# Group normalisation on one core: the next tile's mean ahead of this tile's variance, and the last two stores cut into pieces by rows

## The chip, the core and the metric

The kernel runs on one core of one Trainium2 chip. The metric is the device time of one execution in microseconds (us). Before the change the median of two runs is 732.78 us (732.75 and 732.81). The profile is that of one execution: it lasted 732.78 us, of which the span from the first to the last instruction is 731.1 us.

The engines that matter are TensorE (PE), VectorE (DVE), ScalarE (ACT), and SyncE (SP), which only issues transfers here. Sixteen DMA engines move the data. Each engine works through its own list of instructions in order; semaphores make one engine wait for another.

## What is computed

```python
def reference(x, g, b):
    G = 32
    B, C, H, W = x.shape          # 128, 1024, 32, 16, bfloat16
    xr = x.reshape(B, G, C // G, H, W)
    mu = xr.mean(axis=(2, 3, 4), keepdims=True)
    var = ((xr - mu) ** 2).mean(axis=(2, 3, 4), keepdims=True)
    xn = (xr - mu) / jnp.sqrt(var + 1e-5)
    xn = xn.reshape(B, C, H, W)
    return xn * g[None, :, None, None] + b[None, :, None, None]
```

Each of the 128 samples has 32 groups of 32 channels with 512 pixels each, so one group is 16,384 numbers. Mean and variance are taken over a group; scale and shift go by channel.

## The kernel before

A tile is four samples: 4 x 32 groups make 128 rows (partitions), and a row is one whole group of 16,384 bfloat16 numbers, 32 KB. A tile is thus 4 MB, and there are `NT` = 32 of them. Everything a row needs is in that row. Rows of a tile stand behind one another in memory, in the input as in the output.

The work on tile i is cut into steps, each a small function:

- `L(i)` (line 81) loads the tile into a buffer `xt`, one DMA of 128 rows, issued by SP. There are six such buffers (`XBUFS`), and the first six loads are issued at the start.
- `M(i)` (line 121) is 32 matmuls on PE against the unit matrix `eye`, each on 512 columns of the tile, all added up in one PSUM buffer `ps` of 128 x 512 numbers: the row sum is folded 32 to 1. There are three such buffers.
- `R(i)` (line 137) is one DVE instruction that sums `ps` along the row and gives the negative mean `negmean`. It appears with a second short instruction that reads the accumulator.
- `Q(i)` (line 156) is four ACT instructions on 4,096 columns each. They square x - mean and sum, into the four columns of `sq`.
- `V(i)` turns `sq` into scale and shift: DVE sums the four columns (`jv`, line 173), ACT takes the root (`rstd`, line 186), DVE takes the reciprocal (line 190) and forms `scl` (line 195) and `bia` (line 201), 32 channels each.
- `A(i)` (line 218) is 32 DVE instructions, one for each channel: x times scale plus shift, in place in `xt`.
- `S(i)` (line 229) stores the tile, one DMA of 128 rows, issued by SP.

The order on each engine is written out by hand: `chain` ties each instruction to the one before it on its engine. The main loop goes over the tiles and writes, for tile i: `Q(i)`, `V(i)`, `M(i+1)`, then the first 12 instructions of `A(i)` (`A_HEAD`), then `R(i+1)`, then the other 20 of `A(i)`, then `S(i)`, and then the load `L(i+5)` from i = 1 on. So on DVE the mean of the next tile stands inside the normalisation of this one, behind its first 12 instructions. On ACT `Q(i+1)` stands behind the root of `V(i)`; it reads `negmean` of tile i+1. On SP a store and a load alternate; `S(i)` waits for the last instruction of `A(i)`, and `L(i+5)` goes into the buffer that `S(i-1)` empties, so it waits for that store to land.

Of the kernel before, what the change touches and what calls it, by code (L numbers as in the profile page):

```python
# [18 lines left out]
AHEAD = 5  # L19
MM_FREE = 512  # L20
SQ_FREE = 4096
A_HEAD = 12


@with_exitstack
def kernel(
# [8 lines left out]
    nc = tc.nc  # L35
    P = nc.NUM_PARTITIONS
# [6 lines left out]
    NT = B0 // NS  # L43
    KC = C // G
# [8 lines left out]
    o_v = out.rearrange("(t n) (g k) h w -> t (n g) (k h w)", n=NS, g=G)  # L53
# [16 lines left out]
    def chain(key, inst):  # L70
        prev = last.get(key)
        if prev is not None:
            tc.add_manual_dep(inst.ins, prev.ins.name, nosync, reason="pipeline order")
        last[key] = inst
        return inst

    state = {}

    def L(i):
        xt = xpool.tile([P, F], BF16, name="xt")  # L80
        chain("sp", nc.sync.dma_start(out=xt[:], in_=x_v[i]))
        state[i] = {"xt": xt}
# [11 lines left out]
    for n in range(NS):  # L94
# [7 lines left out]
        out=eye[:],  # L102
        in_=ones_b[:],
# [11 lines left out]
    def M(i):  # L115
        st = state[i]
        ps = pspool.tile([P, MMN], F32, name="ps")
        for k in range(NMM):
            chain(
                "pe",  # L120
                nc.tensor.matmul(  # L121
                    out=ps[:],
                    lhsT=eye[:],
                    rhs=st["xt"][:, k * MMN : (k + 1) * MMN],
                    start=(k == 0),
                    stop=(k == NMM - 1),
                ),
            )
        st["ps"] = ps

    def R(i):
        st = state[i]
        negmean = spool.tile([P, 1], F32, name="negmean")
        jd = jpool.tile([P, MMN], BF16, name="jd")
        chain(
            "dve",
            nc.vector.tensor_scalar(  # L137
                out=jd[:],
                in0=st["ps"][:],
                scalar1=-inv_n,  # L140
                scalar2=None,
                op0=ALU.mult,
                op1=ALU.add,
                accum_out=negmean[:],
            ),
        )
        st["negmean"] = negmean

    def Q(i):
        st = state[i]  # L150
        sq = spool.tile([P, NSQ], F32, name="sq")
        for k in range(NSQ):
            ja = jpool.tile([P, SQ_FREE], BF16, name="ja")
            chain(
                "act",
                nc.scalar.activation(  # L156
                    out=ja[:],
                    in_=st["xt"][:, k * SQ_FREE : (k + 1) * SQ_FREE],
                    func=ACT.Square,
                    bias=st["negmean"][:],  # L160
                    scale=1.0,
                    accum_out=sq[:, k : k + 1],
                ),
            )
        st["sq"] = sq

    def V(i):
        st = state[i]
        var = spool.tile([P, 1], F32, name="var")
        jv = spool.tile([P, NSQ], F32, name="jv")  # L170
        chain(
            "dve",
            nc.vector.tensor_scalar(  # L173
                out=jv[:],
                in0=st["sq"][:],
                scalar1=inv_n,
                scalar2=None,
                op0=ALU.mult,
                op1=ALU.add,
                accum_out=var[:],  # L180
            ),
        )
        rstd = spool.tile([P, 1], F32, name="rstd")
        chain(
            "act",
            nc.scalar.activation(  # L186
                out=rstd[:], in_=var[:], func=ACT.Sqrt, bias=eps_t[:], scale=1.0
            ),
        )
        chain("dve", nc.vector.reciprocal(out=rstd[:], in_=rstd[:]))  # L190
        scl = spool.tile([P, KC], F32, name="scl")
        bia = spool.tile([P, KC], F32, name="bia")
        chain(
            "dve",
            nc.vector.tensor_scalar(  # L195
                out=scl[:], in0=gam[:], scalar1=rstd[:], scalar2=None, op0=ALU.mult
            ),
        )
        chain(
            "dve",  # L200
            nc.vector.scalar_tensor_tensor(  # L201
                out=bia[:],
                in0=scl[:],
                scalar=st["negmean"][:],
                in1=bet[:],
                op0=ALU.mult,
                op1=ALU.add,
            ),
        )
        st["scl"], st["bia"] = scl, bia  # L210

    def A(i, lo, hi):
        st = state[i]
        xt = st["xt"]
        for k in range(lo, hi):
            chain(
                "dve",
                nc.vector.tensor_scalar(  # L218
                    out=xt[:, k * HW : (k + 1) * HW],
                    in0=xt[:, k * HW : (k + 1) * HW],  # L220
                    scalar1=st["scl"][:, k : k + 1],
                    scalar2=st["bia"][:, k : k + 1],
                    op0=ALU.mult,
                    op1=ALU.add,
                ),
            )

    def S(i):
        chain("sp", nc.sync.dma_start(out=o_v[i], in_=state[i]["xt"][:]))
        state.pop(i)  # L230

    M(0)
    R(0)
    for i in range(NT):
        Q(i)
        V(i)
        if i + 1 < NT:
            M(i + 1)
        A(i, 0, A_HEAD)
        if i + 1 < NT:  # L240
            R(i + 1)
        A(i, A_HEAD, KC)
        S(i)
        j = i + AHEAD
        if UPFRONT <= j < NT:
            L(j)
# [30 lines left out]
```

## Time and profile before

| | |
|---|---|
| median of two runs | 732.78 us |
| the profiled execution | 732.78 us |
| its span, first to last instruction | 731.1 us |
| ACT busy | 497.5 us, 68% |
| DVE busy | 379.8 us, 52% |
| PE busy | 288.9 us, 40% |
| read from HBM, written to HBM | 134.23 MB, 134.22 MB |
| the transfers' share of 16 DMA engines | 88.7% |

The page names for each group of instructions the line, the engine, the operation, what it writes and reads, how often it ran, its busy time, the mean duration of one in ns, and behind the second bar how long the engine had been idle before it and what ended that. Idle time counts only where the engine in question is the one that others wait for. The small instructions of the variance, which the prediction does not show again, look like this in the costliest groups of the page:

```profile
L173 DVE TENSOR_SCALAR_CACHE_REDUCE jv<-sq 128x4 f32<-128x4 f32 x32 | 5.0, 157 | 293.1 <-ACT ja L156 293.1
L137 DVE TENSOR_SCALAR_CACHE_REDUCE jd<-ps 128x512 bf16<-128x512 f32 x32 | 21.8, 680 | 0.0
L186 ACT ACTIVATE rstd<-var,eps_t 128x1 f32<-128x1 f32 x32 | 9.4, 294 | 7.4 <-DVE jv L173 7.4
```

The last part of the page tells of the DMAs, with the median time from the issue on the queue to the landing of the last byte:

```profile
xt<-in_x_dram SPq DMA_DIRECT2D x32, 4096.0 KB, 21.9
out_dram<-xt SPq DMA_DIRECT2D x32, 4096.0 KB, 12.1
```

### The profile page before, as it was taken

To read this page: it belongs to the slowest core of one execution; us is meant where nothing else is said; L and a number is where in the kernel's file an instruction comes from. 1 tells how busy PE (TensorE), PEld (TensorE's weight loads), DVE (VectorE), ACT (ScalarE), POOL (GpSimd) and SP (SyncE) were. 2 spreads that over 40 slices of the span, in tenths; PEclk is the share of its full clock that TensorE was granted. 3 is DMA by queue.
4 is the path that set the end of the run, shared out by engine and by line. 5 is a ranking of instruction groups with operands and counts; after the bars stand their busy time and mean duration, and the time that the engine had idled before them with its cause. 6 is when DMAs were issued, how large, how long until landed. Compare 5 with 4: busy or idle time off the path is not lost.

```text
span 731.1 us, 3814 instructions
## 1 busy us (share of the span) xinstructions
PE 288.9 (40%) x1024; PEld 113.1 (15%) x1024; DVE 379.8 (52%) x1252; ACT 497.5 (68%) x290; POOL 0.5 (0%) x5
## 2 busy tenths in 40 slices
PE   2874532455543334445323455433344443330000
PEld 0331110122111111112111122111111111110000
DVE  0034466654446665444566544456654445665443
ACT  0267876666787666678766667876666787666670
POOL 0000000000000000000000000000000000000000
PEclk9997656666667667776667766677767776675555
DMA  9998599999999999999999999999999999934555
GB/s 377 431 437 364 229 385 390 403 402 377 397 404 402 373 402 401 402 375 402 402 374 402 402 402 372 403 402 402 373 420 385 378 400 398 401 145 202 229 229 229
DMA packets 9622, 268.70 MB, mean 368 GB/s; under 512 B 1408, under 2 KB 1408, under 8 KB 1408
## 3 DMA queue, kind: packets, MB, share of 16 engines
q1 hardware_dynamic: 9216, 268.44, 88.7%
q8 instruction: 8, 0.13, 0.1%
q14 instruction: 14, 0.11, 0.0%
q10 hardware_dynamic: 384, 0.02, 0.0%
HBM read 134.23 MB, written 134.22 MB: 367 GB/s over the span
## 4 chain that ended last, share of the span: by engine, by line
ACT 68%; DVE 25%; DMA 4%; issue 1%; ACTq 0%; DVEq 0%
ACT ja L156 67%; DVE xt L218 18%; DVE jd L137 3%; DMA bet_b<-in_b_dram 3%; DMA xt<-in_x_dram 2%; ACT rstd L186 1%; DVE bia L201 1%; DVE scl L195 1%; DVE jv L173 1%; DVE rstd L190 1%; ACTq L156 0%; DVEq L272 0%; DVE bet L113 0%
## 5 line engine op out<-in xcount | busy, mean ns | idle before, releaser
L156 ACT ACTIVATE ja<-xt,negmean 128x4096 bf16<-128x4096 bf16 x128 | 474.7, 3708 | 202.2 <-DVE jd L137 199.1
L121 PE MATMUL ps<-xt,eye 128*128 128x512 bf16 x1024 | 288.9, 453 | 356.7 <-DMA xt<-in_x_dram 343.9
L218 DVE TENSOR_SCALAR xt<-xt,scl,bia 128x512 bf16<-128x512 bf16 x1024 | 335.9, 403 | 1.2
L121 PEld LDWEIGHTS <-eye 128*128 128x128 bf16 x1024 | 113.1, 113 | 532.0 <-DMA xt<-in_x_dram 343.4
L173 DVE TENSOR_SCALAR_CACHE_REDUCE jv<-sq 128x4 f32<-128x4 f32 x32 | 5.0, 157 | 293.1 <-ACT ja L156 293.1
L156 ACT ACTIVATION_READ_ACCUMULATOR ja<-xt,negmean 128x1 f32 x128 | 23.9, 187 | 0.0
L137 DVE TENSOR_SCALAR_CACHE_REDUCE jd<-ps 128x512 bf16<-128x512 f32 x32 | 21.8, 680 | 0.0
L186 ACT ACTIVATE rstd<-var,eps_t 128x1 f32<-128x1 f32 x32 | 9.4, 294 | 7.4 <-DVE jv L173 7.4
L112 DVE CAST gam<-gam_b 128x32 f32<-128x32 bf16 x1 | 0.2, 181 | 26.9 <-DMA gam_b<-in_g_dram 26.9
L190 DVE RECIPROCAL rstd<-rstd 128x1 f32<-128x1 f32 x32 | 5.3, 164 | 11.6 <-ACT rstd L186 11.6
L201 DVE SCALAR_TENSOR_TENSOR bia<-scl,negmean,bet 128x32 f32<-128x32 f32 x32 | 8.0, 251 | 1.1
L195 DVE TENSOR_SCALAR scl<-gam,rstd 128x32 f32<-128x32 f32 x32 | 7.7, 242 | 1.1
L173 DVE DVE_READ_ACCUMULATOR jv<-sq 128x1 f32 x32 | 2.6, 83 | 0.0
L137 DVE DVE_READ_ACCUMULATOR jd<-ps 128x1 f32 x32 | 2.5, 79 | 0.0
L113 DVE CAST bet<-bet_b 128x32 f32<-128x32 bf16 x1 | 0.2, 181 | 3.4 <-DMA bet_b<-in_b_dram 3.4
L90 ACT ACT_TABLE_LOAD x1 | 1.3, 1283 | 0.8 <-PEq L261 0.8
L88 DVE MEMSET eps_t<- 128x1 f32 x1 | 0.1, 59 | 0.9 <-PEq L261 0.9
L101 POOL TENSOR_SCALAR_AFFINE_SELECT eye<-ones_b 128x128 bf16<-128x128 bf16 x1 | 0.3, 293 | 0.7 <-DVE ones_b L99 0.7
L90 ACT ACTIVATE warm<-eps_t 128x1 f32<-128x1 f32 x1 | 0.2, 202 | 0.0
L99 DVE MEMSET ones_b<- 128x128 bf16 x1 | 0.2, 165 | 0.0
L261 POOL MEMSET const-bfloat16-1.0<- 128x1 bf16 x1 | 0.1, 101 | 0.0
L261 POOL MEMSET const-uint8-127<- 128x1 uint8 x1 | 0.1, 101 | 0.0
(2 smaller groups left out, 0.2 us busy)
## 6 DMA issues: line engine op xcount, KB each, us to landing
xt<-in_x_dram SPq DMA_DIRECT2D x32, 4096.0 KB, 21.9
out_dram<-xt SPq DMA_DIRECT2D x32, 4096.0 KB, 12.1
gam_b<-in_g_dram ACTq DMA_DIRECT2D x4, 2.0 KB, 15.7
bet_b<-in_b_dram ACTq DMA_DIRECT2D x4, 2.0 KB, 17.1
```

The lines of the kernel that those rows point to most:

```text
L90: chain("act", nc.scalar.activation(out=warm[:], in_=eps_t[:], func=ACT.Sqrt))
L99: nc.vector.memset(ones_b[:], 1.0)
L101: nc.gpsimd.affine_select(out=eye[:], in_=ones_b[:], pattern=[[-1, P]], compare_op=ALU.is_equal, fill=0.0, base=0, channel_multiplier=1,)
L121: nc.tensor.matmul(out=ps[:], lhsT=eye[:], rhs=st["xt"][:, k * MMN : (k + 1) * MMN], start=(k == 0), stop=(k == NMM - 1),),
L137: nc.vector.tensor_scalar(out=jd[:], in0=st["ps"][:], scalar1=-inv_n, scalar2=None, op0=ALU.mult, op1=ALU.add, accum_out=negmean[:],),
L156: nc.scalar.activation(out=ja[:], in_=st["xt"][:, k * SQ_FREE : (k + 1) * SQ_FREE], func=ACT.Square, bias=st["negmean"][:], scale=1.0, acc ...
L173: nc.vector.tensor_scalar(out=jv[:], in0=st["sq"][:], scalar1=inv_n, scalar2=None, op0=ALU.mult, op1=ALU.add, accum_out=var[:],),
L186: nc.scalar.activation(out=rstd[:], in_=var[:], func=ACT.Sqrt, bias=eps_t[:], scale=1.0),
L190: chain("dve", nc.vector.reciprocal(out=rstd[:], in_=rstd[:]))
L195: nc.vector.tensor_scalar(out=scl[:], in0=gam[:], scalar1=rstd[:], scalar2=None, op0=ALU.mult),
L201: nc.vector.scalar_tensor_tensor(out=bia[:], in0=scl[:], scalar=st["negmean"][:], in1=bet[:], op0=ALU.mult, op1=ALU.add,),
L218: nc.vector.tensor_scalar(out=xt[:, k * HW : (k + 1) * HW], in0=xt[:, k * HW : (k + 1) * HW], scalar1=st["scl"][:, k : k + 1], scalar2=st[ ...
```

## The change

Two things are changed. In the main loop, `M(i+1)` and `R(i+1)` now stand ahead of `V(i)`, and `A(i)` is one piece again. In `S`, the stores of the last two tiles are cut into pieces by rows: 112, 7, 5 and 4 rows for tile 30, and 112, 6, 3, 2 and 5 rows for tile 31. What is computed is the same, and so is the number of instructions on PE, DVE and ACT.

```diff
-A_HEAD = 12
...
-    def A(i, lo, hi):
+    def A(i):
         st = state[i]
         xt = st["xt"]
-        for k in range(lo, hi):
+        for k in range(KC):
...
     def S(i):
-        chain("sp", nc.sync.dma_start(out=o_v[i], in_=state[i]["xt"][:]))
+        cuts = {NT - 2: (112, 119, 124, P), NT - 1: (112, 118, 121, 123, P)}.get(i, (P,))
+        lo = 0
+        for hi in cuts:
+            chain(
+                "sp",
+                nc.sync.dma_start(
+                    out=o_v[i][lo:hi, :], in_=state[i]["xt"][lo:hi, :]
+                ),
+            )
+            lo = hi
         state.pop(i)
...
     for i in range(NT):
         Q(i)
-        V(i)
         if i + 1 < NT:
             M(i + 1)
-        A(i, 0, A_HEAD)
-        if i + 1 < NT:
             R(i + 1)
-        A(i, A_HEAD, KC)
+        V(i)
+        A(i)
         S(i)
```

On DVE, from the mean of tile 0 to the variance of tile 1, the order before is this (line 137 is the mean, 173 the first step of the variance, 218 the normalisation; "x12" stands for twelve in a row):

```order
L137 TENSOR_SCALAR jd,negmean<-ps 128x512
L173 TENSOR_SCALAR jv,var<-sq 128x4
L190 RECIPROCAL rstd<-rstd 128x1
L195 TENSOR_SCALAR scl<-gam,rstd 128x32
L201 SCALAR_TENSOR_TENSOR bia<-scl,negmean,bet 128x32
L218 TENSOR_SCALAR xt<-xt,scl,bia 128x512 x12
L137 TENSOR_SCALAR jd,negmean<-ps 128x512
L218 TENSOR_SCALAR xt<-xt,scl,bia 128x512 x20
L173 TENSOR_SCALAR jv,var<-sq 128x4
```

The same stretch of DVE now, where all lines of the kernel are one lower:

```order
L136 TENSOR_SCALAR jd,negmean<-ps 128x512 x2
L172 TENSOR_SCALAR jv,var<-sq 128x4
L189 RECIPROCAL rstd<-rstd 128x1
L194 TENSOR_SCALAR scl<-gam,rstd 128x32
L200 SCALAR_TENSOR_TENSOR bia<-scl,negmean,bet 128x32
L217 TENSOR_SCALAR xt<-xt,scl,bia 128x512 x32
L136 TENSOR_SCALAR jd,negmean<-ps 128x512
L172 TENSOR_SCALAR jv,var<-sq 128x4
```

The mean of tile 1 has moved ahead of the variance of tile 0 (the "x2"), and the mean of tile 2 stands between the normalisation of tile 0 and the variance of tile 1.

On SP, the end of the program now, from the store of tile 26 on, reads as follows; before, the last row of it was five stores of 128 rows:

```order
L233 DMA out_dram<-xt 128x16384
L80 DMA xt<-in_x_dram 128x16384
L233 DMA out_dram<-xt 128x16384 x3
L233 DMA out_dram<-xt 112x16384
L233 DMA out_dram<-xt 7x16384
L233 DMA out_dram<-xt 5x16384
L233 DMA out_dram<-xt 4x16384
L233 DMA out_dram<-xt 112x16384
L233 DMA out_dram<-xt 6x16384
L233 DMA out_dram<-xt 3x16384
L233 DMA out_dram<-xt 2x16384
L233 DMA out_dram<-xt 5x16384
```

Two DMAs have become nine; the stores and loads ahead of them stand as they did.

## The prediction

> **What bounds the kernel now.** I read the chain of work that ended last first, then the costliest groups, then one tile on DVE and ACT in the timeline, and only then the DMA engines. The line of the chain by engine, and three groups:
>
> ```profile
> ACT 68%; DVE 25%; DMA 4%; issue 1%; ACTq 0%; DVEq 0%
> ...
> L156 ACT ACTIVATE ja<-xt,negmean 128x4096 bf16<-128x4096 bf16 x128 | 474.7, 3708 | 202.2 <-DVE jd L137 199.1
> L121 PE MATMUL ps<-xt,eye 128*128 128x512 bf16 x1024 | 288.9, 453 | 356.7 <-DMA xt<-in_x_dram 343.9
> L218 DVE TENSOR_SCALAR xt<-xt,scl,bia 128x512 bf16<-128x512 bf16 x1024 | 335.9, 403 | 1.2
> ```
>
> ACT is 68% of the chain, and the squares (line 156) sat idle for 199.1 us because the mean (line 137, DVE) came late. The DVE share of the chain, 25%, is what stands ahead of that mean. One tile in the timeline, DVE first, then ACT (start, duration, instruction; idle time before it and its releaser in brackets):
>
> ```profile
> 47.76 0.16 DVE L173 TENSOR_SCALAR_CACHE_REDUCE jv<-sq 128x4 f32<-128x4 f32 x1 [15.37 <-ACT ja L156]
> ...
> 49.05 3.97 DVE L218 TENSOR_SCALAR xt<-xt,scl,bia 128x512 bf16<-128x512 bf16 x12
> 52.93 0.68 DVE L137 TENSOR_SCALAR_CACHE_REDUCE jd<-ps 128x512 bf16<-128x512 f32 x1
> ...
> 53.54 6.54 DVE L218 TENSOR_SCALAR xt<-xt,scl,bia 128x512 bf16<-128x512 bf16 x20
> 69.04 0.16 DVE L173 TENSOR_SCALAR_CACHE_REDUCE jv<-sq 128x4 f32<-128x4 f32 x1 [8.96 <-ACT ja L156]
> ```
> ```profile
> 32.42 3.71 ACT L156 ACTIVATE ja<-xt,negmean 128x4096 bf16<-128x4096 bf16 x1 [30.12 <-DVE jd L137]
> ...
> 36.26 3.71 ACT L156 ACTIVATE ja<-xt,negmean 128x4096 bf16<-128x4096 bf16 x1
> ...
> 47.95 0.29 ACT L186 ACTIVATE rstd<-var,eps_t 128x1 f32<-128x1 f32 x1 [0.23 <-DVE jv L173]
> 53.71 3.71 ACT L156 ACTIVATE ja<-xt,negmean 128x4096 bf16<-128x4096 bf16 x1 [5.46 <-DVE jd L137]
> ```
>
> A tile takes 69.04 - 47.76 = 21.28 us, and it is one serial loop: squares 15.33 us on ACT (32.42 to 47.76), variance 1.29 us (47.76 to 49.05), twelve normalisations 3.97, the mean 0.68, and the squares of the next tile. ACT stands idle 5.46 us before them. The DMA engines are nearly full beside that loop. Three windows of the trace (columns: the engines' busy us, PE clock, the mean busy share of 16 DMA engines, GB/s): loads alone, the steady middle, one store alone:
>
> ```profile
> 14.00:38.00 24.00, 21.28 (x80) 8.65 (x79) 0.97 (x4) 5.55 (x3) 0.00 (x0) 0.93 1.01 433
> ...
> 170.00:584.00 414.00, 179.14 (x634) 69.91 (x632) 228.97 (x756) 300.16 (x176) 0.00 (x0) 0.71 0.96 394
> 719.00:731.00 12.00, 0.00 (x0) 0.00 (x0) 0.12 (x1) 0.00 (x0) 0.00 (x0) 0.50 0.82 350
> ```
>
> The middle has a share of 0.96 already. So I expect a gain in the middle of the few per cent that the DMA engines have left, and the larger part at the ends, where they have room.
>
> **Mean ahead of variance.** No instruction is added or taken away on PE, DVE or ACT. `R(i+1)`, 0.68 us, runs while ACT is still squaring tile i, when DVE is idle (8.96 us in the row above). Behind the squares there remain the first step of the variance and the root, then the next squares: a tile would cost ACT 15.33 + (48.26 - 47.76) = 15.8 us. DVE needs 0.7 + 1.3 + 3.97 + 6.54 = 12.5 us, so it is not the bound; that no longer 12 but all 32 normalisations lie beside the squares costs nothing, since 20 of them did before at 6.54 / 20 = 0.327 us each against 3.97 / 12 = 0.331 alone. A compute loop of 15.8 us is faster than the DMA engines, so the next wait is for loads: the step is set by one store and one load, 8.39 MB.
>
> The change adds a wait too. `R(i+1)` needs `M(i+1)` and so load i+1; behind it on DVE stand `V(i)` and `A(i)`, and behind these `S(i)` and `L(i+5)` on SP. A normalisation in one piece and the matmuls behind the last load:
>
> ```profile
> 708.70 10.42 DVE L218 TENSOR_SCALAR xt<-xt,scl,bia 128x512 bf16<-128x512 bf16 x32
> ```
> ```profile
> 636.87 8.73 PE L121 MATMUL ps<-xt,eye 128*128 128x512 bf16 x32 [12.64 <-DMA xt<-in_x_dram]
> ```
>
> From the landing of load i+1 to the issue of load i+5 that is about 8.7 (matmuls) + 0.7 + 1.3 + 10.4, or 21 us; with the 21.8 us of the next store and load (below) 43 us for four tiles, against four steps of over 80. It doesn't bind.
>
> **How long is the step of a full queue?** Before shows no queue that holds stores and loads throughout; I bound it. One pair in the middle (12.1 is its store, 21.4 its load), the issues of the first store and of the last, and how long the last took:
>
> ```profile
> L229 SPq DMA_DIRECT2D out_dram<-xt x1: 332/332/332, 145.2 to 145.2; - x1
> L81 SPq DMA_DIRECT2D xt<-in_x_dram x1: 383/383/383, 145.6 to 145.6; - x1
> ...
> DMA to landing us min/median/max: 12.1/16.7/21.4
> ```
> ```profile
> 60.11 0.34 SPq L229 DMA_DIRECT2D out_dram<-xt  x1
> ```
> ```profile
> 719.15 0.33 SPq L229 DMA_DIRECT2D out_dram<-xt  x1
> ```
> ```profile
> DMA to landing us min/median/max: 11.1/11.1/11.1
> ```
>
> From the store's issue to the load's landing 145.6 + 21.4 - 145.2 = 21.8 us pass. A store alone takes 11.1, while 4.19 MB at the 433 GB/s of loads alone take 9.7, so 1.4 us are latency that a queue hides: the pair moves in 20.4 us. The share gives the same: 0.96 x 21.28 = 20.4. Lower bound: 2 x 9.7 = 19.4, with no loss where a store gives way to a load. Upper bound: 21.8, nothing hidden. I take 20.5, nearest to the two readings, with 0.1 for the turn from load to store.
>
> To that comes one late DMA engine. Matmuls of tiles 2, 3 and 4 start as their loads land, and instruction fetches are in the DMA table:
>
> ```profile
> 32.84 8.65 PE L121 MATMUL ps<-xt,eye 128*128 128x512 bf16 x32 [2.72 <-DMA xt<-in_x_dram]
> 43.98 7.08 PE L121 MATMUL ps<-xt,eye 128*128 128x512 bf16 x32 [2.50 <-DMA xt<-in_x_dram]
> 53.71 8.47 PE L121 MATMUL ps<-xt,eye 128*128 128x512 bf16 x32 [2.64 <-DMA xt<-in_x_dram]
> ```
> ```profile
> q8 instruction: 8, 0.13, 0.1%
> ```
> ```profile
> q8 instruction: 1, 0.02, 4.0%
> ```
>
> The second of these rows is from a window of 39.0 to 40.7 us, the first from the whole page. 9.73 us is the step of 53.71; that of 43.98 is 11.14, and the packet of queue 8 fell into it. So a fetch makes one DMA engine some 1.4 us late, and it stays late while the queue is full. Eight fetches in 32 tiles are one in four: 0.35 us a tile if they always meet the same engine, 0 if they spread. Before, the pause between pairs took that up. I take the full 0.35, since a load has landed only with its last engine: a step of 20.85 us.
>
> **The two stores in pieces.** 128 rows on 16 engines are 8 rows each, 9.7 / 8 = 1.2 us a row. The 112 rows are 7 each. If the 16 other rows meet idle engines, the fullest still has 8: cost 0. If the four small pieces of the last store all begin on the same engine, it has 11: +3.7. If the engine that is late has 7 rows twice, it saves up to 2 x 1.2 = 2.4. So from -2.4 to +3.7; I take +2.0, nearer to the upper end, since small pieces that start alike pile up and lateness is caught up partly while nothing is loaded. Nine issues for two, 0.33 us of SP each, lie beside the transfers. [...]
>
> **The sum**, on the profiled execution. ACT is free of tile 0 at 48.26; squares of tile 1 to 63.6, variance to 64.9, normalisation (10.42) to 75.3.
>
> - Store of tile 1 issued at 75.4. From there 26 pairs (tiles 1 to 26 with loads 6 to 31) of 20.85 = 542.1, and 1.4 of latency: load 31 lands at 618.9 (before 636.9, when the last matmuls start).
> - Tile 31: matmuls 8.7, mean 0.7, squares 15.4, variance 1.3, normalisation 10.4 = 36.5: its store is issued at 655.4. Stores 27 to 30 (4 x 9.7) are through on the late engine at about 658, on the others well before.
> - That store 11.1, pieces 2.0: 668.5. Before, 719.15 + 11.1 = 730.2 stands against a span of 731.1: 0.9 more. The execution's 732.78 is 1.7 over its span, and equals the median of the runs. Together 671.1, so **671 us**.
>
> Where the 62 us come from: store 1 goes out 6 us earlier (before, 60.1 + 21.28 = 81.4), 26 steps give 26 x 0.43 = 11, and after the last load 36.5 us replace the 719.15 - 636.87 = 82.3 in which before still worked off its backlog; the pieces take 2 back.
>
> **Rivals.** (1) A full queue loses nothing and the fetches spread: a step of 19.4 gives 671 - 26 x 1.45 = 633. The 433 GB/s of loads alone speak for it; the pair's 21.8 us against it. (2) Queues that are never empty cost more: fetches of the other engines also hit, or engines drift apart. A step of 21.3 to 22.5 gives 683 to 714. The late load above speaks for it; against it that before keeps 21.28 with a pause in every step. (3) Not faster: with stores and loads always both in flight, the mixed rate falls. Faster ends at 718 us, so at a step of 22.7, or 370 GB/s; slower by 2%, 747 us, begins at 23.8, or 353 GB/s. The place would be the middle, the price 26 times the excess. The windows, with 394 GB/s at 96%, speak against it. [...] (4) The new wait of `V(i)` for load i+1 binds: the loop above would have to be twice as long; the step would stay near 21.3 or more, and the time 683 or over. That the edit does nothing is excluded by the order of DVE's instructions, which has changed.
>
> **How the numbers follow.** Forecast 0.72 (650 to 685 us), rival 1 0.12 (625 to 650), rival 2 with 4 0.11 (685 to 718), rival 3 0.05. The range takes the forecast and the near parts of both neighbours, 645 to 688. Two per cent is about what a measurement of this kernel can tell from no change: faster 0.95, same 0.03 and slower 0.02, these two from rival 3.
>
> **What would show it.** Right: idle time before the squares released by the mean's late matmuls, hence by loads; in the middle a DMA share at or above 1.0, near 405 GB/s, and the landing times of stores and loads grown by the queue; the chain no longer alternating ACT and DVE but with DMA as its largest part; load 31 near 619 and store 31 issued 36 us after it. Wrong: a step of 21 us or more with the share below 0.97 (the compute loop still bound), or the last store's pieces landing over 15 us after its first issue.

## The result, and the profile after

| | before | changed |
|---|---|---|
| median | 732.78 us (2 runs) | 657.25 us (657.0 and 657.5) |
| ratio, with 95% interval | 1 | 0.8969 [0.8948, 0.8991] |
| span of the profiled execution | 731.1 us | 655.3 us (execution 657.0) |
| DMA share of the 16 engines, 170 to 584 us | 0.96 | 1.00 |

The change makes the kernel 10.3% faster. The forecast was 671, the range 645 to 688. The time lies inside it, but two terms of the sum were off, in opposite directions: by -26 and by +12 us. Most of what follows is about these two.

The chain of the changed kernel by engine, and the groups that answer to those shown of before:

```profile
DMA 61%; ACT 21%; PE 8%; DVE 4%; issue 1%; DVEq 0%; SPq 0%
...
L155 ACT ACTIVATE ja<-xt,negmean 128x4096 bf16<-128x4096 bf16 x128 | 474.2, 3704 | 33.0 <-DVE jd L136 29.9
...
L136 DVE TENSOR_SCALAR_CACHE_REDUCE jd<-ps 128x512 bf16<-128x512 f32 x32 | 22.0, 688 | 157.2 <-PE ps L120 149.5
L185 ACT ACTIVATE rstd<-var,eps_t 128x1 f32<-128x1 f32 x32 | 9.4, 294 | 90.6 <-DVE jv L172 90.6
```

ACT's idle time before the squares has shrunk from 202.2 to 33.0 us, and 29.9 of these are one wait at the start of the program. The mean itself now waits, 149.5 us for matmuls, which wait for loads. Since the variance stands behind that mean on DVE, ACT's remaining wait has moved to the root: 90.6 us, for 7.4 before. The chain no longer changes between ACT and DVE; 61% of it is DMA. SP's own waits say what the DMAs wait for (who waited for whom, us in total, times, longest):

```profile
SPq L80 <- DMA out_dram<-xt: 407.0, 24, 19.8
```

A load has to wait until the store before last has emptied its buffer. Before, that store had landed by then, and SP's wait was for the normalisation (670.8 us for the 32 stores; 168.8 now). In the middle the queue is never empty. The windows of the end and of the middle (the last two columns are the DMA share and GB/s):

```profile
598.00:654.00 56.00, 3.60 (x17) 1.45 (x15) 23.10 (x76) 15.69 (x10) 0.00 (x0) 0.58 0.69 262
170.00:584.00 414.00, 195.32 (x659) 76.00 (x672) 250.79 (x827) 328.42 (x193) 0.00 (x0) 0.70 1.00 431
```

431 GB/s with stores and loads mixed is the rate of loads alone (433). The end is poor: 0.69 and 262 GB/s from 598 us on. Behind the last load, the chain in order of time, and the issue of the last store's five pieces on SP:

```profile
592.62 3.17 PE ps L120 x7
...
619.26 6.87 DVE xt L217 x21
```
```profile
L233 SPq DMA_DIRECT2D out_dram<-xt x5: 261/1187/1905, 629.7 to 638.7; - x5
```

Load 31 lands at 592.6, 26 us earlier than forecast. The first piece of the last store goes out at 629.7, 37.1 us later (forecast: 36.5). The last piece lands at 655.3 - 0.9 = 654.4, so the last store took 24.7 us; 13.1 were forecast, and a whole store on idle engines takes 11.1. SP needed 0.26 to 1.9 us for each of the five issues, where the prediction had 0.33; they went out over 9 us.

### The profile page after: what moved, and what is told of

Read it like the earlier page. It is cut to its first block, busy times and chain, and to the rows that moved or that the text cites. A ratio compares the mean times of both kernels' runs of the same rounds, so it can differ in the third digit from the quotient of the medians.

```text
span 655.3 us, 3802 instructions
## 1 busy us (share of the span) xinstructions
PE 288.2 (44%) x1004; PEld 113.7 (17%) x1024; DVE 380.2 (58%) x1252; ACT 494.1 (75%) x290; POOL 0.5 (0%) x5
## 4 chain that ended last, share of the span: by engine, by line
DMA 61%; ACT 21%; PE 8%; DVE 4%; issue 1%; DVEq 0%; SPq 0%
DMA out_dram<-xt 30%; DMA xt<-in_x_dram 29%; ACT ja L155 21%; PE ps L120 8%; DVE xt L217 3%; DMA bet_b<-in_b_dram 3%; DVE jd L136 1%; DVE jv L172 0%; ACT rstd L185 0%; DVE bia L200 0%; DVE scl L194 0%; DVE rstd L189 0%; DVEq L278 0%; DVE bet L112 0%; SPq L80 0%
## 5 line engine op out<-in xcount | busy, mean ns | idle before, releaser
L155 ACT ACTIVATE ja<-xt,negmean 128x4096 bf16<-128x4096 bf16 x128 | 474.2, 3704 | 33.0 <-DVE jd L136 29.9
L136 DVE TENSOR_SCALAR_CACHE_REDUCE jd<-ps 128x512 bf16<-128x512 f32 x32 | 22.0, 688 | 157.2 <-PE ps L120 149.5
L185 ACT ACTIVATE rstd<-var,eps_t 128x1 f32<-128x1 f32 x32 | 9.4, 294 | 90.6 <-DVE jv L172 90.6
## 6 DMA issues: line engine op xcount, KB each, us to landing
xt<-in_x_dram SPq DMA_DIRECT2D x32, 4096.0 KB, 29.9
```

The lines of the kernel that those rows point to most:

```text
L136: nc.vector.tensor_scalar(out=jd[:], in0=st["ps"][:], scalar1=-inv_n, scalar2=None, op0=ALU.mult, op1=ALU.add, accum_out=negmean[:],),
L155: nc.scalar.activation(out=ja[:], in_=st["xt"][:, k * SQ_FREE : (k + 1) * SQ_FREE], func=ACT.Square, bias=st["negmean"][:], scale=1.0, acc ...
L185: nc.scalar.activation(out=rstd[:], in_=var[:], func=ACT.Sqrt, bias=eps_t[:], scale=1.0),
```

## The experiments

**The two parts apart.** The new order with whole stores:

```diff
-        cuts = {NT - 2: (112, 119, 124, P), NT - 1: (112, 118, 121, 123, P)}.get(i, (P,))
...
+        chain("sp", nc.sync.dma_start(out=o_v[i], in_=state[i]["xt"][:]))
```

> The changed order with whole stores, no cuts. In the changed kernel's trace load 31 lands at 592.6 us and the last store is issued at 629.7 but lands at 654.4, with many packets of 2.4 us, twice the usual 1.21, from the moment the first piece of 112 rows moves. Theory A (the cuts slow the transfers beside them): whole stores go at 9.7 us each, so the late DMA engine is through five of them at 592.6 + 5 x 9.7 = 641.1 and the time is 641.1 + 0.4 + 0.9 + 1.7 = 644 us. Theory B (only rows count: the late engine, which had 19 rows of the last two tiles where 16 are its share, saves three rows): 657.2 - 3 x 1.21 = 653.6 us. Theory C (the cuts help): over 657 us. As predicted (the pieces cost 2.0): 655 us.

Measured: 643.99 us (642.96 to 644.84), ratio 0.8787 [0.8774, 0.8800]. Theory A. The last load lands about where it did in the changed kernel, the last store is issued 1.5 us later, and it takes 11.1 us again (the chain, then the store on SP with its time to landing):

```profile
593.42 9.69 PE ps L120 x32
```
```profile
L228 SPq DMA_DIRECT2D out_dram<-xt x1: 332/332/332, 631.2 to 631.2; - x1
...
DMA to landing us min/median/max: 11.1/11.1/11.1
```

So the order alone is worth 89 us, and the cuts take 13 of them back (657.25 against 643.99). The old order with the cuts:

```diff
-        chain("sp", nc.sync.dma_start(out=o_v[i], in_=state[i]["xt"][:]))
+        cuts = {NT - 2: (112, 119, 124, P), NT - 1: (112, 118, 121, 123, P)}.get(i, (P,))
...
+                    out=o_v[i][lo:hi, :], in_=state[i]["xt"][lo:hi, :]
```

> The old order with the cut stores, so that each of the last two stores starts on idle DMA engines. Theory B (only rows count): the fullest engine has 11 rows for 8, the last store lands 11.1 + 3.7 = 14.8 us after its issue, time 732.8 + 3.7 = 736.5 us. Theory A (pieces of 112 rows make engines stand in one another's way): the store lands later than 15 us, 16 to 20, time 738 to 742 us. Cuts help: 732 us or less.

Measured: 743.72 us (743.65 to 744.5), ratio 1.0151 [1.0136, 1.0166]: 10.9 us slower than before on the same chip (732.83), more than theory A's 738 to 742 and three times the 3.7 us of the rows. The five issues on SP in this trace:

```profile
L234 SPq DMA_DIRECT2D out_dram<-xt x5: 317/908/1888, 719.2 to 722.8; - x5
```

The span is 742.0, so the last piece lands at 741.1, 21.9 us after the first issue.

**Why cut stores are slow.** If only the number of rows an engine moves counted, a cut into 112 and 16 rows would be free, with 7 + 1 rows on each of 16 engines:

```diff
-        cuts = {NT - 2: (112, 119, 124, P), NT - 1: (112, 118, 121, 123, P)}.get(i, (P,))
+        cuts = {NT - 2: (112, P), NT - 1: (112, P)}.get(i, (P,))
```

> The changed order with the last two stores cut into 112 and 16 rows only: each of 16 engines has 7 and 1 rows, 8 in all, as in a whole store. Theory B (only rows count): the time of whole stores, 644 us if the first kernel of this call shows that. Theory A (the 112 rows are dealt to the engines in another way than 128, and engines get in one another's way): packets of 2.4 us again, time clearly above whole stores, 648 to 655 us.

Measured: 655.22 us (653.7 to 655.5), 11 us over whole stores. Of the 13 us that the cuts cost, 11 are there without any piece under 16 rows. The two DMAs of the last store, and their times to landing:

```profile
L233 SPq DMA_DIRECT2D out_dram<-xt x2: 317/1054/1792, 630.6 to 631.0; - x2
...
DMA to landing us min/median/max: 20.9/21.3/21.7
```

In the old order the last five stores each start on idle engines, so five cuts can be measured in one run:

```diff
-        chain("sp", nc.sync.dma_start(out=o_v[i], in_=state[i]["xt"][:]))
+        cuts = {27: (64, P), 28: (112, P), 29: (96, P)}.get(i, (P,))
+        cols = {30: (F // 2, F)}.get(i, (F,))
...
+                        out=o_v[i][lo:hi, c0:c1], in_=xt[lo:hi, c0:c1]
```

> The old order, in which each of the last five stores starts on idle DMA engines, and each is cut in another way: tile 27 into 64 + 64 rows, 28 into 112 + 16, 29 into 96 + 32, 30 into two halves of the columns (128 rows each), 31 whole. Each engine has 8 rows' worth in all five. Rows-only theory: each is through some 11.1 to 12 us after its first issue. [...]

Measured, one run, for tiles 27 and 28 (issues, then times to landing):

```profile
L238 SPq DMA_DIRECT2D out_dram<-xt x2: 549/564/578, 635.1 to 635.7; - x2
...
DMA to landing us min/median/max: 12.1/16.6/21.1
```
```profile
L238 SPq DMA_DIRECT2D out_dram<-xt x2: 352/387/422, 656.4 to 656.8; - x2
...
DMA to landing us min/median/max: 13.0/14.3/15.6
```

From the first issue to the last landing:

```
tile   cut            expected by rows   measured
27     64 + 64 rows   11.1 to 12         635.7 + 21.1 - 635.1 = 21.7
28     112 + 16       11.1 to 12         656.8 + 15.6 - 656.4 = 16.0
29     96 + 32        11.1 to 12         16.3
30     half columns   -                  6.3 each
31     whole          11.1               11.1
```

Tile 27 went out while load 31 was still landing (until 637.0 us, 1.9 us behind its first issue), so its 21.7 us may be a little long. For the column halves 11.1 to 12 us together doesn't apply: each half is released by its own half of the normalisation, so the first was on its way 5 us before the second. Each took 6.3 us, half the 9.7 us of a tile and 1.4 of latency, with no loss. The three cuts by rows speak against the rows-only theory: 128 rows take 16.0 to 21.7 us in two DMAs and 11.1 in one, and the five pieces of tile 31 in the old order took 21.9. The trace of the changed kernel shows slow packets. Of the 264 packets of 32 KB that start from 613.9 us on, about when the first piece is issued, 42 took over 2.0 us; of the 4,740 between 200 and 560 us none did, and their mean is 1.22 us. No row of the trace names an engine, so why cut stores have slow packets was not shown. The prediction counted only rows for each engine, and this is where its second error lies.

**Who is late.** The trace holds 16 landings for each whole load and store, as many as the profile counts DMA engines; I read them as one from each, and their spread as the lateness of the last engine. The prediction had put this down to fetches of PE's instructions. Three kernels with whole stores change what PE or DVE fetch. A quarter of the matmuls:

```diff
-        for k in range(NMM):
+        for k in range(0, NMM, 4):
...
-                    stop=(k == NMM - 1),
+                    stop=(k == NMM - 4),
```

> The changed order with whole stores, and 8 of the 32 matmuls of each tile (every fourth 512 columns; the mean is formed from a quarter of the row). PE then fetches a quarter of the instructions, 2 fetches for 8. Fetch theory (each fetch of PE's instructions makes one and the same DMA engine 1.4 us late while the queue is full): the last DMA engine is 3 us behind the first at load 31, for 11 before, load 31 lands near 584.6 us, and the time is about 584.6 + 48.5 + 0.4 + 2.6 = 636 us. Rival (that engine is slow for another reason): load 31 still lands near 592 us, and the time is that of the first kernel of this call, about 644, since the stores behind load 31 and not the matmuls of tile 31 set the end.

Measured: 643.25 us (642.33 to 644.2), which is not distinguishable from 643.99, and lateness 10.2 us, where the fetch theory had 3. The rival: PE's fetches are not what makes the last engine late. (Why it is 10.2 and not 11.9 stays open.) More DVE instructions:

```diff
+    pad = consts.tile([P, 1], F32)
...
         S(i)
+        for _ in range(32):
+            chain("dve", nc.vector.memset(pad[:], 0.0))
```

> The changed order with whole stores, and 32 tiny DVE instructions (one number a row, into a scratch buffer) behind the normalisation of each tile: DVE runs nearly twice the instructions, for about 2 us a tile, which it has free. Theory: the last DMA engine is late by fetches of 8 KB of DVE's instructions, 1.0 us each, one in three tiles; with one in under two tiles its lateness at load 31 grows from 12 to about 19 us, and the time from 644 to about 652 us. Rival (lateness has another cause): 644 us, lateness 11 to 12 us.

Measured: 649.59 us (649.23 to 649.92), lateness 15.6 us. The right way, but smaller than expected: 5.6 us of the 8 in time, 3.7 of the 7 in lateness. Fewer DVE instructions, with every second channel left unnormalised:

```diff
-        for k in range(KC):
+        for k in range(0, KC, 2):
```

> The changed order with whole stores, and only every second channel normalised (the others are stored as they were loaded): 23 instead of 39 DVE instructions a tile, and a normalisation of 5.2 instead of 10.4 us. Theory (the last DMA engine is late by fetches of DVE's instructions): its lateness at load 31 falls from 12 to about 8 us, and the time by these 4 us, to 640 us, since the stores on that engine set the end. Rival (its lateness has another cause): 12 us as with all channels, and 644 us, since a shorter normalisation alone doesn't help stores that wait for that engine.

Measured: 634.99 us (633.79 to 635.84), lateness 6.9 us. The theory again: 5.0 us less lateness, for the 4 expected. The time fell by 9 us, not 4: with a shorter normalisation the second store also goes out earlier (70.2 us for 75.2), into a gap that the experiment before the last shows below. The four kernels side by side (queues 8 and 14 are instruction fetches; the step is the time from load 6 to load 31 by 25, for the engine that lands first and the one that lands last):

```
kernel            DVE instr.  packets    late at   step of engine
                  a tile      q8   q14   load 31   first   last
whole stores      39          8    14    11.9 us   19.36   19.83
few matmuls       39          2    15    10.2      19.38   19.77
more DVE          71          8    22    15.6      19.37   19.91
half normalised   23          8    10     6.9      19.37   19.56
```

In the second half of the run with whole stores the lateness grows by 1.0 us in every third tile and stays: 8.0, 8.0, 8.0, 8.9, 9.0, 8.9, 9.9 and on. That is once in 3 x 39 = 117 DVE instructions. With 23 instructions a tile its last two growths, at loads 25 and 30, are five tiles apart, 115 instructions. From load 14 to load 31 the count comes to one us for 99, 108, 134 and 128 DVE instructions in the four kernels of the table. The packets of queue 14 agree in time: with whole stores they start at 352.1, 411.1, 470.2, 529.2 and 587.1 us, and the loads at which the lateness grows (19, 22, 25, 28 and 31) have their last landing at 357.1, 416.2, 475.2, 534.3 and 593.4. Other packets of that queue (at 489.5, for one) leave the last engine as it was. The trace names no engine, but steps that all add up on the last landing speak for one and the same DMA engine that carries these fetches of DVE, each of which makes it 1 us late for good in a queue that never empties (a DMA share of 1.00).

The landings also show where PE's fetches go. With whole stores, 10 of the 16 engines land load 18 within 0.6 us of the first; 9 do so at load 19, 8 at load 23, 7 at load 27 and 6 at load 31. Each time a packet of queue 8 starts shortly before (343.0, 422.6, 501.5 and 580.0 us). With a quarter of the matmuls it is 10 at load 18 and 9 at load 31, and the one packet of queue 8 between them, at 497.2, stands before that one drop. So each of these fetches of PE makes another engine late: they spread, which the prediction had priced at 0.

The last engine sets the end in all four kernels: from its landing of load 31 to the last landing of the program 48.3 to 49.1 us pass, about the five stores of 9.7 us that are left by then. In the run with whole stores the compute behind load 31 and the last store alone, 37.8 + 11.1 us, come to the same.

**The step of a full queue.** The first engine's step of 19.4 us is 2 x 9.7, with no loss where a store gives way to a load; the prediction had 20.5. Is that loss tied to every turn, or to a queue that has run empty? The old order with 8 normalisations ahead of the mean has a compute loop between the two:

```diff
-A_HEAD = 12
+A_HEAD = 8
```

> The old order with 8 instead of 12 normalisations ahead of the next mean, whole stores: a compute loop of 21.28 - 4 x 0.33 = 19.96 us. Theory A (a store followed by a load costs nothing more than 2 x 9.7 us where the queue is never empty; only a pause makes the turn cost): the compute loop still sets the step, 19.96 us, time 732.8 - 31 x 1.32 = 692 us. Theory B (the turn from store to load costs about 1.1 us in every step, as the prediction took it): step 20.5 us, time 732.8 - 31 x 0.78 = 709 us.

Measured: 692.77 us (692.73 to 692.94), ratio 0.9453 [0.9439, 0.9467]. Theory A to 1 us. The stores and loads go out every 20 us, less than the 20.4 us that the pair was thought to need:

```profile
299.87 0.33 SPq L229 DMA_DIRECT2D out_dram<-xt  x1
...
319.85 0.33 SPq L229 DMA_DIRECT2D out_dram<-xt  x1
```

So a turn from store to load does not cost 1.1 us of itself: with a shorter pause a pair fits into 20.0 us. The packets say the same. Between 200 and 560 us a packet of 32 KB takes 1.27 us on average before the change, 1.25 with 8 ahead and 1.22 with whole stores in the new order; 16 of them, one pair's share of an engine, make 20.4, 20.0 and 19.5 us. That all engines turn at the same moment does not explain the slower packets by itself: in the run with whole stores load 7 lands 19.4 us after load 6, while 13 of the 16 engines are within 0.4 us of one another. What makes them slow in the old order stays open.

With 4 ahead of the mean:

```diff
-A_HEAD = 12
+A_HEAD = 4
```

> The old order with 4 normalisations ahead of the next mean, whole stores: a compute loop of 21.28 - 8 x 0.33 = 18.6 us, shorter than the 19.4 us of a full queue. Theory (the place of the mean matters only until the compute loop is shorter than the transfers of a tile): the time of the new order with whole stores, 644 us, within 1%. Rival (the mean has to be ahead of the variance): 732.8 - 31 x 2.64 = 651 us or more.

Measured: 652.76 us (652.7 to 652.86). That is 1.4% over 644. Here my theory fell, and the rival, the compute loop of 18.6 us all the way, was right. Loads did come at the pace of the full queue, and load 31 was there at 594.97, when its matmuls start. But its mean ran only at 611.29, 7.2 us after the last of them:

```profile
594.97 9.11 PE L121 MATMUL ps<-xt,eye 128*128 128x512 bf16 x32 [10.81 <-DMA xt<-in_x_dram]
```
```profile
611.29 0.68 DVE L137 TENSOR_SCALAR_CACHE_REDUCE jd<-ps 128x512 bf16<-128x512 f32 x1
```

Six tiles are loaded ahead of the first store. A loop that is only 0.8 us a tile faster than the DMA has not worked that lead off by the last load: the mean still waits for the variance of the tile before.

**A faster kernel.** In the changed kernel, as in the one with whole stores, the DMA engines have a gap near 70 us: the second store goes out at 75, when the first is through. The squares of tile 0 wait until 32.4 us, because two conversions of scale and shift, whose small loads land at 31.6, stand ahead of the first mean on DVE. Moved behind it, with the new order and whole stores:

```diff
-    nc.vector.tensor_copy(out=gam[:], in_=gam_b[:])
-    nc.vector.tensor_copy(out=bet[:], in_=bet_b[:])
...
     M(0)
     R(0)
+    chain("dve", nc.vector.tensor_copy(out=gam[:], in_=gam_b[:]))
+    chain("dve", nc.vector.tensor_copy(out=bet[:], in_=bet_b[:]))
```

> The changed order with whole stores, and the two conversions of scale and shift to float32, which wait for small loads until 31.6 us, behind the first mean on DVE instead of ahead of it. Squares of tile 0 then start at about 22.7 us, not 32.4, and store 1 goes out near 66 us instead of 75, before the first store is through: the DMA engines don't run empty between the first two stores (3.6 us) and the turn behind it costs nothing (0.9). Theory (from there on the DMA queue alone sets the time): 4.5 us less, 639.5 us. Rival (the end is set by compute behind load 31, or the gap is made up elsewhere): 644 us.

Measured: 636.85 us (636.5 to 637.07), ratio 0.8689 [0.8676, 0.8702], 7.1 us under whole stores, where the theory had 4.5, and the fastest kernel of the study with the whole computation, together with the next. The squares of tile 0 start at 24.0 us (22.7 expected) and store 1 goes out at 66.8 (66 expected); load 31 lands 6.3 us earlier than with whole stores on the first engine and 7.8 on the last. Why that is more than 4.5 was not followed up. GB/s by slices, changed kernel first, then this one; the fifth slice is the gap:

```profile
GB/s 385 417 445 416 293 388 444 423 436 427 436 423 434 433 428 434 426 436 428 436 422 437 428 432 432 436 430 434 431 433 433 428 437 430 436 430 435 326 268 82
```
```profile
GB/s 368 426 428 426 432 427 425 434 434 424 436 426 434 434 430 429 429 436 427 434 430 433 430 438 430 432 435 434 434 428 434 431 432 434 432 438 432 429 339 273
```

Last, the final store of that kernel in two halves by columns:

```diff
-        chain("sp", nc.sync.dma_start(out=o_v[i], in_=state[i]["xt"][:]))
+        cols = {NT - 1: (F // 2, F)}.get(i, (F,))
...
+            chain("sp", nc.sync.dma_start(out=o_v[i][:, c0:c1], in_=xt[:, c0:c1]))
```

> The kernel with the conversions behind the first mean, and the last store in two halves by columns, each of 128 rows, the first of which goes out after half of the normalisation. Theory (the last DMA engine, some 10 us late, is what the end waits for: there store 30 lands at 624.4 us, after which 9.7 us of rows remain): no gain worth naming, 635 to 637 us. Rival (the last store starts on idle engines, and a half of it lands in 6.3 us instead of 11.1): 632 us.

Measured: 637.15 us (636.35 to 637.17): no gain, as the theory had it. The halves land 11.0 and 10.6 us after their issues, where 6.3 would do on idle engines.

## Why the prediction was right, and where it was wrong

Its steps against the changed kernel's profiled execution (657.0 us):

```
step                                   forecast   measured   off
store of tile 1 issued                  75.4       75.0      -0.4
load 31 lands                          618.9      592.6     -25.9 from there
store 31 issued after it                36.5       37.1      +0.6
last store to its last landing          13.1       24.7     +11.6
end of the span, outside the span        2.6        2.6       0
sum                                    671.1      657.0     -14.1
```

- *The serial loop goes, and the wait for loads takes its place.* Right, with the sign and the kind of the next wait: mean behind matmuls behind loads, and the chain with DMA as its largest part. The place was off by one instruction: the idle time that the prediction expected before the squares stands before the root of the tile ahead (90.6 us), since the variance is behind the mean on DVE.
- *The new wait of the variance for load i+1 doesn't bind.* Right: the DMA engines move 431 GB/s in the middle, the rate of loads alone, so no load is issued too late for them. The compute behind the last load was right too, 37.1 us for 36.5.
- *A step of 20.5 us for a pair in a full queue.* Wrong, and the larger error: 19.4 us on the first engine. I took a value near the middle of the bounds, 19.4 and 21.8, because two readings agreed on 20.4. Both were readings of a queue that runs empty once a tile, the very condition that the change removes; the second (0.96 x 21.28) counts slow packets, 1.27 us for 1.22, as busy. Rival 1, at 0.12, had this right, and also that fetches spread, as PE's do; it lacked the late engine.
- *0.35 us a tile for a late engine.* The size held roughly (19.83 - 19.36 = 0.47 with whole stores), and so did lateness that is never made up. The culprit did not: PE's fetches spread over the engines, and it is DVE's that meet the same one. That the size came out near is luck.
- *The pieces: +2.0, between -2.4 and +3.7.* Wrong in kind: 13 us in the changed kernel, 10.9 alone. The prediction's own sign of being wrong, pieces landing over 15 us after the first issue, came: 24.7 us. The bounds counted rows for each engine, and no row of before could show more, since all loads and stores of tiles there have 128 rows. No run shows the term of +2.0; what the runs show in its place is that cuts by rows slow the transfer itself, 16.0 to 21.7 us for 11.1. The upper bound of +3.7 supposed small pieces that begin on the same engine, and in part they met: the last landing comes 5 to 10 us behind the one before it in the changed kernel's pieces of 7, 6, 5 and 4 rows, and 0.7 and 1.0 us in those of 3 and 2, as if the late engine had rows of the former alone. But this was the smaller effect.

That the time came within 14 us of the forecast is partly luck: with the first error alone it would have been 645, at the edge of the range, with the second alone 683.

## What to carry to other kernels

When a change turns a loop bound by compute into one bound by transfers, the transfers' price has to be read where their queue is full (the six loads at the start, here, at 9.7 us each), not where it drains once in each step (20.4 us for a pair that took 19.4), even if the DMA share there is 0.96. Cutting a 128-row transfer by rows nearly doubled its time, with not a row more to move (64 + 64 rows: 21.7 us for 11.1). A cut by columns cost nothing that the runs could show (637.15 us for 636.85) and lets the first half go early (5.1 us there). And with a queue that never empties, look at the last of the 16 engines: what made it late here added up to 11.9 us by the last load, and from there to the end.

## What the runs showed that I had not expected

Instruction fetches of one compute engine helped set the end of a kernel bound by transfers: about 1 us for each 99 to 134 DVE instructions, as far as the landings tell always on the same DMA engine, 6.9 to 15.6 us by the last load. With 16 fewer instructions a tile on an engine that is 42% idle, that DMA engine was 5.0 us less late at the last load. PE's fetches met another engine each time, as far as the landings tell: with whole stores the engines within 0.6 us of the first fell from 10 to 6 over four of them.
